# Twelve result stores begun by GpSimd in place of SyncE

## The chip, the cores and the metric

The kernel runs on one core of a Trainium2 chip. A core has five engines that each work through their own list of instructions in order: TensorE (PE in the profile), VectorE (DVE), ScalarE (ACT), GpSimd (POOL) and SyncE (SP). They meet at semaphores. The metric is device time in microseconds (us) of one execution.

## What is computed

Three stages follow one another. Attention through 32 memory slots for each of 4 batches and 8 heads gives `x`; a two-layer block with a sloped rectifier maps it; and a gated mixture of four experts, all of them evaluated, gives the result:

```
a    = softmax(phi);  k_m = a^T k;  v_m = a^T v            # per batch and head
attn = softmax(q k_m^T / 8) v_m                            # -> x, 2304 x 512
h    = x @ w_in;  g = max(h, 0) + alpha * min(h, 0);  x = g @ w_out
p    = domain_probs / sum(domain_probs)
for e in range(4):
    out += p[:, e] * (max(x @ w1[e], 0) @ w2[e])           # w1 512 x 1024, w2 1024 x 512
```

The result has 2304 rows (576 for each batch) and 512 columns, in float32.

## The kernel before

Products are done in three passes: each operand is split into a rounded high half and a low half (the rest), and high x high, high x low and low x high are summed. ScalarE makes the high half (a cast), VectorE or GpSimd the low half (a subtraction). So nearly every operand of TensorE passes two engines first. In a product of six matrix instructions the third and the sixth use the low half of the weights, the second and the fifth the low half of the other operand.

The expert stage cuts the four experts into eight groups `g` of 512 hidden columns, and takes batches in pairs: batches 0 and 1 for all eight groups, then batches 2 and 3. Both layers are done as 2 x 2 block products with seven multiplications in place of eight (Strassen's scheme). For the second layer (class `Seven`) a batch keeps seven sums P1 to P7 over all groups in SBUF, the tiles `acc`, and only at the end are these combined into the four blocks of the result: function `combine` (L1086 to L1097), seven additions of 128x576, of which four end in a block that is stored. Batches 0 to 2 store from `combine`, 288 KB a store, four for each batch; batch 3 ends in another form, and its eight stores of 144 KB come from `Down.flush` (L1018).

The order of all instructions is written out by hand in `ORDER` (L30), one name for a step; each engine gets its own steps in that order. `cb01` is the combination number 1 of batch 0; numbers 1, 4, 5 and 6 store. `ON_VECTOR` names the steps that VectorE does in place of GpSimd; of the combinations `cb03`, `cb11`, `cb14` and five of batch 3 are GpSimd's, the rest VectorE's. Batch 0 and batch 1 are combined between 727 and 773 us, interleaved with the first group of batches 2 and 3 and with the last group of batch 1; batch 2 at the end, between the last products of batch 3.

Names used below: `vl711` is the subtraction for the low half of the second-layer weight tile `w2711` of the last group; `D70_13` is a product of group 7, batch 0, that uses it (tile `c7013`). `x3l5` fills the low half of one of the seven first-layer operands of batch 3 (second half of tile `x36`), and `p4_030` uses it. `S02_4` is the difference for a second-layer operand of group 0, batch 2 (it is written to `h020`), `H02_4` and `H02_2` are casts (ScalarE), `L02_2` a subtraction, and `D02_4` the product behind them (tile `c024`). All subtractions of halves stand in one helper, so they carry its line, L324. The buffers of `acc` for batches 0 and 1 are used again for 2 and 3; the first write there waits until the stores have landed.

Of the kernel before, what the change touches and what calls it, by code (L numbers as in the profile page):

```python
# [288 lines left out]
def memory_attention_experts(ctx: ExitStack, tc: tile.TileContext, phi, q, kv, w_in, w_out, w1, w2, alpha, dp, out):  # L289


    nc = tc.nc
# [27 lines left out]
    def engine(name):  # L320
        return nc.vector if name in ON_VECTOR else nc.gpsimd
# [764 lines left out]
    def combine(b, n):  # L1086

        o, x, y, op = (
            (P6, P1, P6, ALU.add), (P2, P1, P2, ALU.add), (P7, P6, P7, ALU.add), (P6, P6, P5, ALU.add),
            (P3, P6, P3, ALU.add), (P4, P7, P4, ALU.subtract), (P5, P7, P5, ALU.add),  # L1090
        )[n]
        a = acc_t[b]
        engine(f"cb{b}{n}").tensor_tensor(out=a[o], in0=a[x], in1=a[y], op=op)
        if b < 3 and o in (P2, P3, P4, P5):
            i, j = divmod((P2, P3, P4, P5).index(o), 2)
            rows = out[i * 256:(i + 1) * 256, b * S + j * HB:b * S + (j + 1) * HB]
            nc.sync.dma_start(out=rows.rearrange("(m p) n -> p m n", p=128), in_=a[o])  # L1097

    def plan_experts():

# [76 lines left out]
        def do_combine(b, n):  # L1177
            do(f"cb{b}{n}", combine, b, n)
# [409 lines left out]
```

## Time and profile before

| | us |
|---|---|
| median of 3 runs | 1100.97 |
| lowest, highest | 1100.07, 1102.19 |
| the profiled execution | 1100.15 |
| its span, from first to last instruction | 1098.4 |

| engine | busy us | share |
|---|---|---|
| TensorE (PE) | 1089.1 | 99% |
| its weight loads (PEld) | 1055.4 | 96% |
| VectorE (DVE) | 804.6 | 73% |
| ScalarE (ACT) | 562.1 | 51% |
| GpSimd (POOL) | 548.3 | 50% |

The shares are means over the span. Transfers: 185.40 MB in 62584 packets, all issued by SyncE but for instruction fetches; the 16 DMA engines were busy for 47.9% with these. In the order of time a row is a run of like instructions on one engine: its start, the time from its first to its last, line, operation and tiles, their count, and in brackets how long the engine was idle before it and what ended that. SPq is SyncE's queue: only the issue is shown there, and the transfer goes on behind it.

### The profile page before, as it was taken

The page shows a single profiled execution, that of the slowest core. Times are in us where ns is not written, and L with a number is a line of the kernel's source. Part 1 is how long each engine was busy: PE and PEld are TensorE (multiplying, and loading weights), DVE is VectorE, ACT ScalarE, POOL GpSimd, SP SyncE. Part 2 cuts the span into 40 slices and gives each one's busy share as a digit, 9 for nine tenths or more (in the row PEclk, how much of TensorE's full clock was granted, in tenths as well). Part 3 has the DMA queues.
Part 4 walks back from the last instruction along what each step waited for, and adds up shares of the span by engine and source line. Part 5 has one row for each costly group of instructions (what it writes and reads, how often), then busy time and mean ns, then how long its engine had stood idle before and what let it go on. Part 6 is the DMA issues. An engine that isn't in the chain of part 4 may idle for free.

```text
span 1098.4 us, 22039 instructions
## 1 busy us (share of the span) xinstructions
PE 1089.1 (99%) x8550; PEld 1055.4 (96%) x8550; DVE 804.6 (73%) x1520; ACT 562.1 (51%) x1236; POOL 548.3 (50%) x443
## 2 busy tenths in 40 slices
PE   9999999999999999999999999999999999999998
PEld 8679999999999999999999999999999999999998
DVE  6987787767556778788788888888466666656556
ACT  5676654544444466665766666765523232333231
POOL 3656545533435466467665554544433333354572
PEclk9999999999999999999999999999999999999999
DMA  9930221201011438566646665778655564555542
GB/s 375 395 149 20 81 75 59 77 22 59 1 52 37 154 137 306 198 235 260 203 198 225 252 233 188 266 239 287 192 182 166 163 193 154 176 164 165 184 144 87
DMA packets 62584, 185.40 MB, mean 169 GB/s; under 512 B 6288, under 2 KB 24720, under 8 KB 58768
## 3 DMA queue, kind: packets, MB, share of 16 engines
q1 hardware_dynamic: 62480, 184.00, 47.9%
q8 instruction: 67, 1.10, 0.4%
q14 instruction: 37, 0.30, 0.1%
HBM read 117.62 MB, written 66.36 MB: 167 GB/s over the span
## 4 chain that ended last, share of the span: by engine, by line
PE 96%; DVE 2%; DMA 1%; issue 0%; SPq 0%; POOL 0%; ACT 0%; DVEq 0%; POOLq 0%
PE c L1064 30%; PE y L705 18%; PE uy L899 13%; PE uw L899 9%; PE ux L899 9%; PE h L671 9%; PE y L702 1%; PE pw L630 1%; PE warm L337 1%; PE o L1010 1%; PE pm L439 1%; PE h L668 1%; DMA w2c<-kS 1%; DMA w<-kw 1%; PE pc L471 0%; DVE h L1037 0%
## 5 line engine op out<-in xcount | busy, mean ns | idle before, releaser
L324 POOL TENSOR_TENSOR gc<-h,gc 128x576 fp32r<-128x576 f32 x102 | 149.5, 1473 | 204.7 <-ACT gc L1045 204.3
L705 PE MATMUL y<-g,wout 128*128 128x288 f32 x1440 | 205.5, 296 | 0.0
L705 PEld LDWEIGHTS y<-g,wout 128*128 128x128 f32 x1440 | 195.4, 188 | 7.3 <-ACT g L690 2.5
L1045 ACT CAST gc<-h 128x576 fp32r<-128x576 f32 x217 | 142.9, 674 | 115.0 <-DVE h L1037 69.8
L1064 PE MATMUL c<-gc,w2c 128*128 128x288 f32 x1260 | 192.3, 295 | 0.9 <-DMA w2c<-kS 0.9
L1084 DVE TENSOR_TENSOR acc<-c,acc 128x288 f32<-128x288 f32 x280 | 124.2, 453 | 83.5 <-PE c L1064 83.0
L899 PE MATMUL uy<-x,w 128*128 128x288 f32 x1152 | 183.1, 295 | 0.2 <-DMA w<-kw 0.2
L1064 PEld LDWEIGHTS c<-gc,w2c 128*128 128x128 f32 x1260 | 175.3, 188 | 1.3 <-ACT gc L1045 1.1
L899 PEld LDWEIGHTS uy<-x,w 128*128 128x128 f32 x1152 | 163.0, 188 | 0.4 <-ACT v L971 0.4
L324 POOL TENSOR_TENSOR g<-act,g 128x288 fp32r<-128x288 f32 x81 | 70.3, 875 | 123.6 <-ACT g L690 92.6
L899 PE MATMUL uw<-x,w 128*128 128x288 f32 x768 | 122.9, 296 | 0.2
L899 PE MATMUL ux<-x,w 128*128 128x288 f32 x768 | 121.7, 295 | 0.0
L1064 PE MATMUL c<-gc,sS 128*128 128x288 f32 x768 | 117.8, 295 | 1.1 <-DVE acc L1084 1.1
L671 PE MATMUL h<-a,wp 128*128 128x288 f32 x720 | 110.2, 296 | 0.0
L899 PEld LDWEIGHTS uw<-x,w 128*128 128x128 f32 x768 | 108.7, 188 | 0.9 <-DVE ux L936 0.6
L899 PEld LDWEIGHTS ux<-x,w 128*128 128x128 f32 x768 | 108.7, 188 | 0.0
L324 DVE TENSOR_TENSOR gc<-h,gc 128x576 fp32r<-128x576 f32 x115 | 100.5, 883 | 10.9 <-ACT gc L1045 10.7
L1064 PEld LDWEIGHTS c<-gc,sS 128*128 128x128 f32 x768 | 106.9, 188 | 1.4 <-DVE acc L1084 1.4
L686 DVE SCALAR_TENSOR_TENSOR act<-neg,bet,h 128x288 f32<-128x288 f32 x120 | 60.3, 510 | 63.9 <-ACT neg L677 57.4
L671 PEld LDWEIGHTS h<-a,wp 128*128 128x128 f32 x720 | 99.9, 188 | 5.7 <-issue 2.3
L677 ACT ACTIVATE neg<-h 128x288 f32<-128x288 f32 x128 | 52.1, 411 | 98.0 <-PE h L671 95.5
L1082 ACT COPY acc<-c 128x288 f32<-128x288 f32 x154 | 60.3, 401 | 75.1 <-PE c L1064 74.1
(160 smaller groups left out, 1618.3 us busy)
## 6 DMA issues: line engine op xcount, KB each, us to landing
kw<-w SPq DMA_DIRECT2D x16, 1792.0 KB, 8.2
raww<-in_w SPq DMA_DIRECT2D x32, 512.0 KB, 4.2
kS<-sS SPq DMA_DIRECT2D x32, 512.0 KB, 5.7
w<-kw SPq DMA_DIRECT2D x32, 512.0 KB, 4.8
w2c<-kS SPq DMA_DIRECT2D x32, 512.0 KB, 3.8
kw<-w SPq DMA_DIRECT2D x25, 512.0 KB, 5.9
w<-kw SPq DMA_DIRECT2D x48, 256.0 KB, 4.2
w2c<-kw SPq DMA_DIRECT2D x24, 512.0 KB, 3.7
```

What stands on the lines that cost most here:

```text
L324: eng.tensor_tensor(out=out, in0=in0, in1=in1.bitcast(F32), op=ALU.subtract)
L337: mm(p[:, 0:128], ident, ident, start=True, stop=True)
L439: mm(p[32 * h:32 * h + 32, 0:128], l, r, start=(c == 0), stop=(c == 4))
L671: mm(p, wp_t[b, c, g][:, x, fs], a_t[b][:, y, g, o:o + HB], start=(n == 0), stop=(n == 5))
L677: nc.scalar.activation(out=self.neg, in_=self.p, func=AF.Relu, scale=-1.0)
L686: nc.vector.scalar_tensor_tensor(out=self.g, in0=self.neg, scalar=bet[:, ft:ft + 1], in1=self.p, op0=ALU.mult, op1=ALU.add)
L705: mm(First.acc[d], w[:, x, d * 128:(d + 1) * 128], self.gt[:, y, 0:HB], start=(self.start and n == 0), stop=(self.stop and n == 2))
L899: mm(p, w[:, x, a, k], operand(self.b, i)[:, y, k], start=(start and n == 0), stop=(n == 5), skip_group_check=not start)
L1045: nc.scalar.copy(out=t[:, 0], in_=self.raw(q))
L1064: mm(p, w[:, x, i, m * 128:(m + 1) * 128], self.g_t[q][:, y, i], start=(fresh and k == 0), stop=(k == 5), skip_group_check=not fresh)
L1082: nc.scalar.copy(out=a, in_=self.ps[n])
L1084: nc.vector.tensor_tensor(out=a, in0=self.ps[n], in1=a, op=ALU.add)
```

## The change

One line of `combine`: the stores of the combined blocks are issued by GpSimd in place of SyncE. The steps, their order in `ORDER`, the additions and the bytes are the same.

```
@@ -1094,7 +1094,7 @@
         if b < 3 and o in (P2, P3, P4, P5):
             i, j = divmod((P2, P3, P4, P5).index(o), 2)
             rows = out[i * 256:(i + 1) * 256, b * S + j * HB:b * S + (j + 1) * HB]
-            nc.sync.dma_start(out=rows.rearrange("(m p) n -> p m n", p=128), in_=a[o])
+            nc.gpsimd.dma_start(out=rows.rearrange("(m p) n -> p m n", p=128), in_=a[o])
```

The order of instructions on GpSimd, first place: around the first store (`cb01`). `w2711` is the weight tile of `vl711`, `x30` an operand tile of batches 2 and 3, `acc0` the block that is stored.

```order
 L767 TENSOR_TENSOR xt23_9566<-yu211_9146,yu201_8524 128x576 [waits DVE_49,Pool_49]
 L1037 TENSOR_TENSOR h710_9369<-h711_9481,h710_9369 128x576 [waits DVE_49]
+L1097 DMA out_0<-acc0_5207 128x2x288 [waits DVE_49,Activation_49]
 L324 TENSOR_TENSOR w2711_9409<-raww215_9031,w2711_9409 128x512 [waits DMAHW1_49]
 L324 TENSOR_TENSOR x30_9604<-yu211_9146,x30_9604 128x576 [waits Activation_49]
```

The store, with its wait for VectorE's sum, now stands ahead of the subtraction for `w2711`.

GpSimd, second place: the other stores of batch 0 and the first of batch 1. `x36` is the tile of `x3l5`, the first `h020` row the difference `S02_4` or the one after it, `acc1` batch 1's block.

```order
 L1037 TENSOR_TENSOR h020_9674<-h020_9674 128x576 [waits DVE_49]
-L767 TENSOR_TENSOR xt32_9883<-yu310_9676,xt31_9798 128x576 [waits DMAHW4_49,DVE_49]
+L1097 DMA out_0<-acc0_5207 128x2x288 [waits DVE_49]
+L767 TENSOR_TENSOR xt32_9883<-yu310_9676,xt31_9798 128x576 [waits DMAHW3_49,Pool_49]
+L1097 DMA out_0<-acc0_5207 128x2x288 [waits DVE_49] x2
 L324 TENSOR_TENSOR x36_9863<-xt32_9883,x36_9863 128x576 [waits Activation_49]
+L1037 TENSOR_TENSOR h020_9674<-h021_9727,h020_9674 128x576
+L1093 TENSOR_TENSOR acc1_5524<-acc10_5525,acc1_5524 128x576
+L1097 DMA out_0<-acc1_5524 128x2x288 [waits Pool_49]
 L1037 TENSOR_TENSOR h020_9674<-h021_9727,h020_9674 128x576 [waits DVE_49]
```

Two stores in a row now stand ahead of `x36` and of the first of the two `h020` differences (`S02_4`).

SyncE, around the fourth and fifth stores: `w2c04` is the weight load with the row at 757.88 us.

```order
 L861 DMA w2c06_9936<-kw2011_5830 128x1024
-L1097 DMA out_0<-acc0_5207 128x2x288
 L827 DMA w170_8872<-kw110_5794 128x2x512
 L827 DMA w171_8992<-kw111_5895 128x2x512
 L827 DMA w170_8872<-kw110_5794 128x2x256
-L1097 DMA out_0<-acc1_5524 128x2x288
 L861 DMA w2c04_10018<-kS30_5751 128x1024
 L861 DMA w2c05_10086<-kS20_5159 128x1024
```

On SyncE the stores are gone, and the loads follow one another in the order that they had.

## Rows read from the trace of the kernel before

**Rows 1.** The page: busy us, share, instructions; the chain that ended last, by engine

```profile
PE 1089.1 (99%) x8550; PEld 1055.4 (96%) x8550; DVE 804.6 (73%) x1520; ACT 562.1 (51%) x1236; POOL 548.3 (50%) x443
...
PE 96%; DVE 2%; DMA 1%; issue 0%; SPq 0%; POOL 0%; ACT 0%; DVEq 0%; POOLq 0%
```

**Rows 2.** Waits of PE: who waited for whom, us in total, times, longest

```profile
PE warm L337 <- POOL ident masks.py:199: 1.4, 1, 1.4
...
PE c L1064 <- DVE acc L1084: 1.1, 1, 1.1
PE c L1064 <- DMA w2c<-kS: 0.9, 1, 0.9
```

**Rows 3.** Line L1097: ns least/median/most, first and last start us; landing

```profile
L1097 SPq EVENT_SEMAPHORE  x12: 17/17/7271, 721.4 to 1094.1; - x12
L1097 SPq DMA_DIRECT2D out<-acc x12: 378/388/541, 728.7 to 1094.4; - x12
...
DMA to landing us min/median/max: 2.3/2.7/7.0
```

**Rows 4.** Order of time, SyncE: start us, us, what

```profile
728.68 0.39 SPq L1097 DMA_DIRECT2D out<-acc  x1
...
757.88 1.05 SPq L861 DMA_DIRECT2D w2c<-kS  x2
...
1094.36 0.38 SPq L1097 DMA_DIRECT2D out<-acc  x1
1095.27 0.33 SPq L1018 DMA_DIRECT2D out<-acc  x1
```

**Rows 5.** Order of time, TensorE

```profile
727.01 1.75 PE L1064 MATMUL c<-gc,w 128*128 128x288 f32 x12
...
754.88 0.97 PE L899 MATMUL uy<-x,w 128*128 128x288 f32 x6
...
757.29 2.67 PE L1064 MATMUL c<-gc,w2c 128*128 128x288 f32 x18
...
765.63 1.03 PE L1064 MATMUL c<-gc,w2c 128*128 128x288 f32 x6 [0.92 <-DMA w2c<-kS]
...
776.03 1.75 PE L1064 MATMUL c<-gc,w2c 128*128 128x288 f32 x12
```

**Rows 6.** Order of time, GpSimd

```profile
721.85 1.81 POOL L324 TENSOR_TENSOR w<-raww,w 128x512 fp32r<-128x512 f32 x1
731.44 1.43 POOL L324 TENSOR_TENSOR x<-yu,x 128x576 fp32r<-128x576 f32 x1 [7.78 <-ACT x L775]
...
749.29 1.43 POOL L324 TENSOR_TENSOR x<-xt,x 128x576 fp32r<-128x576 f32 x1 [3.99 <-ACT x L775]
750.68 1.95 POOL L1037 TENSOR_TENSOR h<-h,h 128x576 f32<-128x576 f32 x1
...
769.56 2.01 POOL L1093 TENSOR_TENSOR acc<-acc,acc 128x576 f32<-128x576 f32 x1 [2.21 <-DVE acc L1093]
```

**Rows 7.** Order of time, VectorE

```profile
727.87 0.75 DVE L1093 TENSOR_TENSOR acc<-acc,acc 128x576 f32<-128x576 f32 x1
...
753.43 1.20 DVE L1093 TENSOR_TENSOR acc<-acc,acc 128x576 f32<-128x576 f32 x1
...
755.41 1.42 DVE L324 TENSOR_TENSOR gc<-h,gc 128x576 fp32r<-128x576 f32 x2
...
768.74 1.54 DVE L1093 TENSOR_TENSOR acc<-acc,acc 128x576 f32<-128x576 f32 x2
```

**Rows 8.** Order of time, ScalarE

```profile
753.78 1.25 ACT L1045 CAST gc<-h 128x576 fp32r<-128x576 f32 x2
...
775.64 0.41 ACT L1082 COPY acc<-c 128x288 f32<-128x288 f32 x1
```

**Rows 9.** DMA issues: count, KB each, median us to landing

```profile
out<-acc SPq DMA_DIRECT2D x8, 144.0 KB, 2.0
```

**Rows 10.** Cores: span, mean granted TensorE clock

```profile
core 0: 1098.4 us, clock 0.999
```

More of the change, by code (lines that the diff above doesn't have):

```diff
@@ L1096, in combine @@
             rows = out[i * 256:(i + 1) * 256, b * S + j * HB:b * S + (j + 1) * HB]
-            nc.sync.dma_start(out=rows.rearrange("(m p) n -> p m n", p=128), in_=a[o])
+            nc.gpsimd.dma_start(out=rows.rearrange("(m p) n -> p m n", p=128), in_=a[o])
     def plan_experts():
```

## The prediction

> **What bounds the kernel now.** I read the page's busy shares and chain of waits first, then TensorE's own waits, then the rows of the stores themselves, then the order of time on SyncE, GpSimd, TensorE, VectorE and ScalarE between 715 and 790 us and after 1090 us. TensorE (PE) is busy for 1089.1 of 1098.4 us and the chain that ends last is 96% PE [rows 1]. So hardly anything can be won: the one wait of PE near these stores is 0.92 us for a weight load, with 1.1 us for VectorE's accumulation before it [rows 2]. A microsecond that PE is made to wait is, on the other hand, nearly always a microsecond of the run, since no later stretch has slack to give it back. The reader should therefore ask what PE waits for, and nothing else.
>
> The twelve stores are cheap where they stand: SyncE (SP) needs 0.38 to 0.54 us to issue one, and they land after 2.3 to 7.0 us, median 2.7 [rows 3]. SP pays with waiting, up to 7.27 us for the first of them, because the block isn't summed yet [rows 3]; but SP only issues transfers and can afford it. In rows 4 the first store goes out at 728.68, right behind the VectorE sum that starts at 727.87 and takes 0.75 [rows 7]: 0.06 us from the end of the sum to the issue. That is my price for one hand-over from engine to engine.
>
> **What the move does.** GpSimd (POOL) works strictly in the order in which its instructions stand. A store put there waits for its sum, and all that stands behind it waits too. So for each of the twelve I asked which POOL instruction stands next and who needs it. Two figures are needed: the time of the sum, which the trace has, and the time for which POOL is held to begin a store, call it g, which it has not, since POOL issues no transfer before. The nearest rows are SP's 0.39 us for the same store [rows 3] and the 1.43 us of a POOL instruction over a block of this size [rows 6]; farther off lie 2.3 us, the shortest landing, if POOL were held till the data are out, and 0 if it only passed the order on. I take 1.0, near the middle of the two nearest, and keep 0.39 to 1.43 as the likely and 0 to 2.3 as the outer bounds. The Trainium skill, "DMA: Bandwidth & Descriptors", section "Specifications", gives about 1 us to the first byte by GpSimd's software path against about 0.6 us by SyncE's; no run here shows it, and by it the sum below would be the same.
>
> **Place 1, +3.5 us.** Behind the first store stands the subtraction that makes the low half of the second-layer weight tile w2711. Before, it ran at 721.85 for 1.81 us, and POOL then had nothing to do until 731.44 [rows 6]. Now it starts when the store has been issued: 728.68 + g, and ends at 730.49 + g. PE wants this tile in the second six of the twelve products at 727.01 [rows 5]; at 1.59/12 = 0.1325 us each (1.75 less the overlap of the last) the third of these six, the first to use the low half, was at 728.07. Wait: 728.68 + g + 1.81 + 0.06 - 728.07 = 2.48 + g = 3.48 us. VectorE's sum doesn't get earlier, since VectorE is busy ahead of it.
>
> **Place 2, +2.8 us.** The third and fourth stores stand directly before the subtraction for the last operand half of batch 3 (x36, before at 749.29) and the difference h020 (before at 750.68) [rows 6]. The fourth store's sum starts on VectorE only at 753.43 [rows 7]; without POOL beside it I give it 0.75 in place of 1.20, so it is done at 754.18, and POOL is through the store at 754.24 + g. Then x36 to 755.67 + g and h020 to 757.10 + g (1.43 each). PE wanted x36 in the third product from 754.88 on, at 755.14 [rows 5], so it waits 0.6 + g there. But the chain from h020 is longer: ScalarE's two casts (1.25 [rows 8]), of which the second doesn't need h020 but stands behind the one that does, VectorE's subtraction (0.71, half of a pair [rows 7]), three hand-overs: 759.24 + g. The products at 757.29 [rows 5] need it from their second on, at 757.42. Both waits together are 1.82 + g = 2.82 us. All this is in the times of before; sum and products shift alike by place 1, so it adds up.
>
> **Place 3, 0.** The stores of batch 1: VectorE's two sums end at 770.28 [rows 7], then store, POOL's own sum (2.01 before, at 769.56 [rows 6]; 1.43 without VectorE beside it) and its store. These land at 770.28 + 2g + 1.43 + (2.7 - 0.39) = 774.0 + 2g. ScalarE needs it at 775.64 [rows 8], as the buffer is written again there, and PE has 0.78 us to spare behind that (ScalarE's end at 776.05, second half of the products of 776.03 at 776.83 [rows 5]). Free up to g = 1.2; 0.5 us at g = 1.43.
>
> **What is saved, -0.9 us.** SP loses twelve issues and its waits. Of that only the 0.92 us at 765.63 [rows 5] reaches PE: the load for it is issued at 757.88 [rows 4], behind a store; now it has the 2.8 us of place 2 besides, so I count the wait as gone. What stands behind the first store in SP's queue (a weight copy, a gate row, weight loads) may go up to 7 us sooner, but PE waits for none of it now [rows 2], so that is worth nothing.
>
> **The end, +0.4 us.** Batch 2's stores find POOL idle. The last goes out at 1094.36 as before [rows 4], and lands at 1094.36 + 2.7 + (g - 0.39) = 1097.67, against 1095.27 + 2.0 = 1097.27 for the last of batch 3 [rows 3, 4, 9].
>
> **Sum**: 3.48 + 2.82 + 0 - 0.92 + 0.4 = 5.8 us on the profiled execution's 1100.15, so 1105.9. That run is 0.8 below the median of 1100.97; against that, 1106.8 us. With g = 0.39: 2.87 + 2.21 - 0.92 = 4.2, with 1.43: 3.91 + 3.25 + 0.5 - 0.92 + 0.8 = 7.5; that is 1105.1 to 1108.5 for the likeliest case.
>
> **A rule that would make g larger.** VectorE does only two-input sums and scaled products around both places, and these slow POOL somewhat: 1.81 to 2.01 us against 1.43 [rows 6]. The Trainium skill, "SBUF - State Buffer", section "Who interferes with whom", says that VectorE's copies, casts and one-input scalar operations can lock GpSimd out while it writes a transfer's descriptors, and that two-input sums don't. By the rule g stays short here. No run shows it yet.
>
> **Rivals.** (a) *Not slower*: the waiting store doesn't hold POOL's queue, or w2711 is somehow ready by 728.07; then nothing new waits, and SP's lighter queue takes away the 0.92: 1100.0. For it: POOL is idle half of the time [rows 1], and 7.8 us of it lie just there [rows 6]. Against: the idle time is behind w2711, and the store ahead of it. It decides at g + 1.81 + 728.68 < 728.07, which not even g = 0 meets. (b) *Held until landing*, g = 2.3: 4.78 + 4.12 + 2.2 - 0.92, and at the end four stores of 2.3 from 1090.2 on, landing near 1099.4 (+2.2): 12.4 us, 1113.4. For it speaks only that no row excludes it. (c) *The clock falls in the wait*. The granted clock is 0.999 in the mean [rows 10], and PE's waits are 1.4 us at most [rows 2]; 3.5 us in one piece don't occur. The missing 0.001 is 1.1 us over the run; one such loss at each place gives 5.8 + 2.2 = 8.0, 1109.0. The Trainium skill, "TensorE: Matmul & The Clock Gate", section "HAM oscillation", describes TensorE going back to 1.2 GHz when it has to wait for data; this trace shows no such case.
>
> **Chances.** Forecast (both waits, g up to 1.43) 0.72; (a) 0.10; (b) 0.08; (c) 0.10. The measurement tells about 0.2%, 2.2 us, from no change. Of the forecast hardly anything lies below that; of (a) most is "same". Faster 0.03, same 0.08, slower 0.89. The range takes in (c), part of (b), and below, g = 0 with a POOL subtraction of 1.43 in place 1 (2.1 + 1.8 - 0.9 = 3.0, 1104.0): 1103.5 to 1111.
>
> **What would show it.** In the changed profile PE waits for POOL's weight subtraction of w2711 (two to four us, nothing of it before), then near 755 + 3.5 us for POOL's x36 and for VectorE behind ScalarE; POOL's idle time before w2711 is put down to VectorE's sum; the wait for w2c at 765 is gone; the times after 790 are those of before plus a constant. It is wrong if w2711 still ends before its store, if a PE wait of this size shows at another place, or if POOL is held far off 1 us by a store.

## The result and the profile after

| | before | after |
|---|---|---|
| median us | 1100.52 (4 runs, 1099.91 to 1102.19) | 1110.09 (4 runs, 1109.28 to 1112.90) |
| the profiled execution | 1100.15 | 1109.79 |
| its span | 1098.4 | 1108.0 |

The ratio is 1.0094, interval 1.0081 to 1.0107. The kernel became slower by 9.6 us, where 5.8 were forecast.

First the page of the kernel after: busy us and share of each engine, and the chain that ended last (before: [rows 1]).

```profile
PE 1091.9 (99%) x8550; PEld 1057.2 (95%) x8550; DVE 808.9 (73%) x1520; ACT 562.4 (51%) x1236; POOL 556.2 (50%) x455
...
q0 software_dynamic: 960, 3.54, 0.9%
...
PE 93%; DVE 3%; issue 1%; DMA 1%; POOL 1%; ACT 0%; POOLq 0%; ACTq 0%; DVEq 0%
```

The twelve stores stand on POOL's list (455 in place of 443) and have a queue of their own (960 packets, 3.54 MB). The chain has given 3% of PE to DVE, POOL and DMA. PE's share says nothing, since a product at half clock counts as busy. PE's waits say more: five are new against [rows 2], of 3.58, 1.65, 0.39, 0.43 and 1.16 us, and the one for w2c of 0.92 us is gone. Where they stand is seen in the order of time on TensorE of the kernel after, with which [rows 5] are to be compared:

```profile
727.23 1.23 PE L1064 MATMUL c<-gc,w 128*128 128x288 f32 x8
732.04 1.20 PE L1064 MATMUL c<-gc,w 128*128 128x288 f32 x4 [3.58 <-POOL w L324]
...
737.38 0.96 PE L899 MATMUL uy<-x,w 128*128 128x288 f32 x6
...
762.43 0.94 PE L899 MATMUL uy<-x,w 128*128 128x288 f32 x5 [1.65 <-POOL x L324]
...
765.88 1.73 PE L1064 MATMUL c<-gc,w2c 128*128 128x288 f32 x11 [0.39 <-DVE gc L324]
768.03 1.07 PE L1064 MATMUL c<-gc,w2c 128*128 128x288 f32 x6 [0.43 <-ACT acc L1082]
768.93 0.96 PE L899 MATMUL uy<-x,w 128*128 128x288 f32 x6
...
784.02 0.96 PE L1064 MATMUL c<-gc,w2c 128*128 128x288 f32 x6
786.14 1.06 PE L1064 MATMUL c<-gc,w2c 128*128 128x288 f32 x6 [1.16 <-ACT acc L1082]
787.04 0.96 PE L899 MATMUL uy<-x,w 128*128 128x288 f32 x6
```

The same three products behind the places on TensorE of the kernel before:

```profile
731.78 0.96 PE L899 MATMUL uy<-x,w 128*128 128x288 f32 x6
...
759.79 0.95 PE L899 MATMUL uy<-x,w 128*128 128x288 f32 x6
...
777.62 0.96 PE L899 MATMUL uy<-x,w 128*128 128x288 f32 x6
```

The sum of the difference is read from such rows: the start of the same product in both traces, at each place. The profiled run of after was 0.22 us late already at 727.23. After that it lost 5.38 us by 737.38 (before 731.78), 3.54 more by 768.93 (before 759.79), gave back 1.15 by 784.02 (before 776.03), where the wait for w2c was, and lost 1.43 by 787.04 (before 777.62). It won 0.37 where PE of the kernel before waits 0.15 us for a weight load, at 1044.14. The end is 0.55 longer: the last issue at 1104.32 is followed by 3.68 us, before by 3.13. Together 0.22 + 5.38 + 3.54 - 1.15 + 1.43 - 0.37 + 0.55 = 9.6.

The windows of the kernel after around place 1 (the stretch, its length, busy us of PE, PEld, DVE, ACT and POOL with their counts, PE's granted clock, DMA share, GB/s) show what the rows of PE alone don't tell:

```profile
730.00:732.00 2.00, 0.00 (x0) 0.00 (x0) 1.22 (x3) 0.00 (x0) 1.97 (x2) 1.00 0.57 147
732.00:734.00 2.00, 1.96 (x8) 1.96 (x9) 0.00 (x0) 0.69 (x2) 0.00 (x0) 0.55 0.98 373
734.00:736.00 2.00, 2.00 (x11) 2.00 (x11) 0.00 (x0) 0.45 (x3) 0.00 (x0) 0.59 0.09 37
736.00:738.00 2.00, 2.00 (x17) 2.00 (x16) 0.42 (x1) 2.00 (x4) 0.95 (x1) 1.00 0.03 8
```

After the wait PE runs for some 3.7 us mostly at the lower of its two levels, 1.2 GHz: 8 and 11 products in 2 us where 17 are usual. Of the 5.38 us of place 1, 3.75 are the wait (the ninth product was due at 727.23 + 8 x 0.1325 = 728.29 and began at 732.04) and 1.63 the clock.

GpSimd in the kernel after, around the first store, the fourth, and the last two of batch 1 (before: [rows 6]):

```profile
729.53 0.87 POOL L1097 DMA_DIRECT2D out<-acc  x1 [7.42 <-DVE h L1037]
730.42 1.57 POOL L324 TENSOR_TENSOR w<-raww,w 128x512 fp32r<-128x512 f32 x1
...
760.21 0.73 POOL L1097 DMA_DIRECT2D out<-acc  x1 [3.62 <-DVE ux L936]
760.97 1.41 POOL L324 TENSOR_TENSOR x<-xt,x 128x576 fp32r<-128x576 f32 x1
762.32 1.43 POOL L1037 TENSOR_TENSOR h<-h,h 128x576 f32<-128x576 f32 x1
...
779.46 0.72 POOL L1097 DMA_DIRECT2D out<-acc  x1 [1.82 <-DVE acc L1093]
780.21 1.45 POOL L1093 TENSOR_TENSOR acc<-acc,acc 128x576 f32<-128x576 f32 x1
782.06 0.73 POOL L1097 DMA_DIRECT2D out<-acc  x1 [0.41 <-POOL acc L1093]
```

w2711 is subtracted behind the store, and the operand of `x3l5` behind the fourth. The line of the stores in the kernel after (before: [rows 3]) gives what GpSimd needs for one, and how long they took to land:

```profile
L1097 POOL DMA_DIRECT2D out<-acc x12: 725/725/872, 729.5 to 1103.8; - x12
...
DMA to landing us min/median/max: 2.6/3.0/7.3
```

ScalarE waited for two of them, in the order of time of the kernel after (before: [rows 8]):

```profile
767.58 0.40 ACT L1082 COPY acc<-c 128x288 f32<-128x288 f32 x1 [2.55 <-DMA out<-acc]
...
785.69 0.40 ACT L1082 COPY acc<-c 128x288 f32<-128x288 f32 x1 [0.73 <-DMA out<-acc]
```

At these two rows the block buffer of batch 0 (of batch 1) is written for the first time by batch 2 (batch 3). Three of the four stored blocks, those of the numbers 1, 4 and 5, lie in one tile (`Seven.flush`, L1076 to L1079), so this write waits until all three stores have landed. The fourth store of batch 0, begun at 760.21, landed 7.27 us later; the last of batch 1 (`cb14`), begun at 782.06, 3.53 us later. Both stand in the chain of waits:

```profile
760.21 7.27 DMA out<-acc
...
782.06 3.53 DMA out<-acc
```

### The profile page after: what moved, and what is told of

It is laid out like the page before. It is cut to its first block, busy times and chain, and to the rows that moved or that the text cites. A ratio compares the mean times of both kernels' runs of the same rounds, so it can differ in the third digit from the quotient of the medians.

```text
span 1108.0 us, 22038 instructions
## 1 busy us (share of the span) xinstructions
PE 1091.9 (99%) x8550; PEld 1057.2 (95%) x8550; DVE 808.9 (73%) x1520; ACT 562.4 (51%) x1236; POOL 556.2 (50%) x455
## 3 DMA queue, kind: packets, MB, share of 16 engines
q0 software_dynamic: 960, 3.54, 0.9%
## 4 chain that ended last, share of the span: by engine, by line
PE 93%; DVE 3%; issue 1%; DMA 1%; POOL 1%; ACT 0%; POOLq 0%; ACTq 0%; DVEq 0%
PE c L1064 29%; PE y L705 17%; PE uy L899 13%; PE uw L899 9%; PE ux L899 9%; PE h L671 9%; PE y L702 1%; PE pw L630 1%; PE warm L337 1%; PE pm L439 1%; DMA out<-acc 1%; PE h L668 1%; DVE gc L324 1%; PE pc L471 0%; DVE acc L1093 0%
## 5 line engine op out<-in xcount | busy, mean ns | idle before, releaser
L324 DVE TENSOR_TENSOR gc<-h,gc 128x576 fp32r<-128x576 f32 x115 | 103.4, 908 | 13.7 <-ACT gc L1045 13.3
```

Of the source, the lines that this page charges most:

```text
L324: eng.tensor_tensor(out=out, in0=in0, in1=in1.bitcast(F32), op=ALU.subtract)
```

## Experiments

Theory A says that a store costs by its place: by what stands behind it on GpSimd while it waits, by the clock after a long wait, and by its landing. Rival B says that a store that GpSimd begins costs about 0.8 us wherever it stands (9.6 / 12). Shifts are read as above, from the same product in two traces; ratios are against the kernel before. Executions start the stretch at 727 us up to 1.0 us apart, so spans alone tell less than shifts.

**The first store back on SyncE.**

```
-            nc.gpsimd.dma_start(out=rows...., in_=a[o])
+            eng = nc.sync if (b, n) == (0, 1) else nc.gpsimd
+            eng.dma_start(out=rows...., in_=a[o])
```

> Only the first store (cb01 of batch 0) goes back to SyncE, the other eleven stay on GpSimd. Theory A (position): a store costs what stands behind it in GpSimd's queue while it waits for its sum; the first one costs 5.4 us of the 9.6 in the profiled runs (3.6 of wait for w2711, the rest at a lower granted clock). So about +4.2 us against before, ratio near 1.0038, no wait of PE for w2711, and granted clock 1.00 in 730 to 740. Rival B (each store has a price of its own, 0.8 us, wherever it stands): +8.8 us, ratio 1.0080.

Measured: ratio 1.0033 (1.0021 to 1.0045), span 1102.4. The shift at place 1 is 0 (731.70 against 731.78), the clock 1.00 throughout. This is as A says.

**The first store alone on GpSimd** (the condition above with `!=`).

> Only the first store is begun by GpSimd, the other eleven by SyncE. A: the whole of place 1, about +5.4 us, ratio near 1.0049, with the wait for w2711 of 3.6 us and the lower clock behind it, nothing at places 2 and 3, and the 0.9 us wait for w2c at 765 still there or hidden by the shift. B: +0.8 us, ratio 1.0007.

Measured: ratio 1.0042 (1.0029 to 1.0055), span 1102.9. One store of twelve costs nearly half of the loss, and B is out. TensorE of this run, and its windows behind the wait:

```profile
731.92 1.06 PE L1064 MATMUL c<-gc,w 128*128 128x288 f32 x4 [3.58 <-POOL w L324]
...
737.26 0.96 PE L899 MATMUL uy<-x,w 128*128 128x288 f32 x6
```

```profile
732.00:734.00 2.00, 2.00 (x10) 2.00 (x11) 0.00 (x0) 0.95 (x3) 0.00 (x0) 0.57 1.05 400
734.00:736.00 2.00, 2.00 (x11) 2.00 (x11) 0.00 (x0) 0.30 (x2) 0.00 (x0) 0.58 0.02 8
```

The stretch began at 727.11, 0.10 late, so the shift by 737.26 is 5.38, as in the kernel after. Of the w2c wait 0.4 us is left.

**The subtraction ahead of the store**, all twelve on GpSimd; in `ORDER`:

```
- ... p6_020 cb01 sk7S3 x3h0 p1_021 S71_6 E70_13 D71_1 F71_1 E71_5 vl711 pg03 D70_13 ...
+ ... p6_020 vl711 cb01 sk7S3 x3h0 p1_021 S71_6 E70_13 D71_1 F71_1 E71_5 pg03 D70_13 ...
```

> All twelve stores are on GpSimd; in the list of steps only the subtraction vl711 is moved ahead of cb01, so that w2711 is made before the store waits. A: place 1 disappears as in the run with the first store on SyncE, about +4.2 us against before (ratio 1.0038), though GpSimd still begins the store. B (or the time of beginning a store is what counts): no change from the changed kernel, +9 us or more.

Measured: ratio 1.0038 (1.0025 to 1.0050), no wait for w2711, clock 1.00. GpSimd still begins the store, and place 1 is free: its price was the order alone.

**Work for TensorE during the wait.** `p5_021` ahead of `D70_13`, and five times over:

```
-            self.product(self.w, V1, T1, True)
+            for _ in range(5 if self.name == "021" else 1):
+                self.product(self.w, V1, T1, True)
```

> All stores on GpSimd as in the changed kernel; the product p5_021 is moved ahead of D70_13 and done five times over (24 more matrix instructions, about 3.2 us, the last pass gives the result), so that PE has work while GpSimd is held by the first store. If the lower clock behind place 1 comes from PE's idle time: the granted clock stays at 1.00 from 730 to 740, the shift against before at 738 to 760 is 3.4 to 4.0 us in place of 5.6, and the run about 8 us over before (1.0073). If the clock falls for another reason (GpSimd's or VectorE's work, the transfer): the low stretch stays, and the run is at least as slow as the changed kernel, 9.6 us or more.

Measured: ratio 1.0076 (1.0062 to 1.0090), span 1106.2, 1.8 us under the kernel after although 24 products more are done; the intervals of the two ratios overlap, so the trace decides. The windows of this run:

```profile
730.00:732.00 2.00, 2.00 (x17) 2.00 (x17) 0.89 (x2) 0.00 (x0) 1.66 (x2) 1.00 0.66 174
732.00:734.00 2.00, 1.86 (x14) 1.63 (x13) 0.00 (x0) 1.31 (x4) 0.00 (x0) 1.00 0.97 375
734.00:736.00 2.00, 2.00 (x17) 2.00 (x16) 0.56 (x2) 2.00 (x5) 1.22 (x1) 1.00 0.05 14
```

GpSimd's store and subtraction are done as in the kernel after (1.66 us of GpSimd in 730 to 732, DMA share 0.66 and 0.97 there and behind); only PE isn't idle, and the clock stays at 1.00. The stretch began at 726.90, 0.11 early, so the shift is 3.57 us, of which 24 x 0.1325 = 3.18 are the added products; the other 0.39 us I can't put down to anything. So the 1.63 us of clock come from PE's idle time.

**Batch 2's four stores alone on GpSimd** (condition `b < 2` for SyncE).

> Only batch 2's four stores, at the end, are begun by GpSimd; the eight of batches 0 and 1 stay on SyncE. A (position): nothing stands behind them that PE waits for, so only the later landing of the last one counts: +0.2 to +0.6 us, ratio 1.0000 to 1.0006, and all times up to 1090 us as before. B (a price for each store, 0.8 us): +3.2 us, ratio 1.0029.

Measured: ratio 1.0006 (0.9997 to 1.0015), no new wait of PE. This is as A says; B's 1.0029 is outside.

**The third and fourth stores back on SyncE** (`cb04`, `cb05` of batch 0).

> The third and fourth stores (cb04 and cb05 of batch 0) go back to SyncE, ten stay on GpSimd. A: place 2 goes, with PE's waits for x36 (1.65 us), for VectorE's gc (0.39) and for ScalarE's acc (0.43): 3.5 us less than the changed kernel, of which up to 1.1 us may come back as the wait for w2c that the changed kernel has lost; +6 to +7.2 us against before (1.0055 to 1.0065). B (0.8 us a store): +8 us (1.0073). If the wait for ScalarE's acc stays, the fourth store lands late because of the traffic and not because GpSimd began it.

Measured: ratio 1.0065 (1.0052 to 1.0078), the upper end of A. B's 1.0073 lies in the interval too, so here the trace decides. PE's waits for x36, gc and ScalarE's acc at 762 to 768 are gone; 0.18 us of the w2c wait came back, and a new wait of 0.60 stands at 758.54, which hangs on VectorE (its two subtractions at 751.41 took 3.19 us; see the run with five stores). The fourth store, on SyncE ahead of the weight loads again, landed after 2.4 us.

**The last two stores of batch 1 back on SyncE** (`cb16`, `cb14`).

> The last two stores of batch 1 (cb16 and cb14) go back to SyncE, ten stay on GpSimd. A: place 3 is paid because GpSimd begins both stores in turn with its own sum between them, so that the last one lands too late for ScalarE's next write of that block; without it PE's wait of 1.16 us near 786 goes, and the run is 1.0 to 1.4 us shorter than the changed kernel's, about +8.3 us against before (1.0075), places 1 and 2 unchanged. Rival: the landing is late because the transfers are crowded by then, whoever begins them: the wait stays, +9 to +9.6 us.

Measured: ratio 1.0073 (1.0060 to 1.0087). PE's wait near 786 is gone, places 1 and 2 stand (3.57 and 1.65 us). That is what A says; the times alone don't exclude the rival, whose 9 us are 1.0082. VectorE's two sums ran as late in this run as in the kernel after (778.09 against 777.49, in a run that was 0.60 later at the product of 768.03), so their lateness alone doesn't make the wait: GpSimd's holding of the two stores is needed for it. Why they are late is seen on VectorE of the kernel before and of the kernel after, just ahead of them:

```profile
764.64 1.42 DVE L324 TENSOR_TENSOR gc<-h,gc 128x576 fp32r<-128x576 f32 x2
...
773.79 2.55 DVE L324 TENSOR_TENSOR gc<-h,gc 128x576 fp32r<-128x576 f32 x2
```

In each run in which GpSimd begins the store of `cb15` in its place, a subtraction of GpSimd stands right behind it (773.60 in the kernel after), and these two of VectorE take 2.44 to 2.56 us; in each run in which SyncE begins it they take 1.42.

**All stores behind the work that PE waits for**, as steps of their own on GpSimd: in `ORDER` `st01` behind `vl711`, `st06` behind `x3t2`, `st04 st05 st11` behind `cb11`, `st15` behind `L02_6`, `st16 st14` behind `cb14`.

```
+    def store(b, n):
+        ...
+        nc.gpsimd.dma_start(out=rows...., in_=acc_t[b][o])
```

> All twelve stores on GpSimd, but as steps of their own, each behind the GpSimd work that PE waits for: the first behind vl711, the third and fourth behind x3l5, S02_4 and cb11, those of batch 1 behind the next operand work. A: GpSimd may begin the stores if nothing waits behind them: the waits of places 1 and 2 go, with at most 1.5 us left where a store that goes out later also lands later before ScalarE's next write of its block: 0 to +1.5 us against before (1.0000 to 1.0014). B (the beginning of a store costs as such): +5 us or more.

Measured: ratio 1.0055 (1.0043 to 1.0068), and this I had wrong. The waits of places 1 and 2 did go, but later stores landed later, and at 780.70 PE waited another 0.74 us for VectorE's gc. ScalarE and TensorE of this run:

```profile
763.27 0.40 ACT L1082 COPY acc<-c 128x288 f32<-128x288 f32 x1 [7.41 <-DMA out<-acc]
...
763.72 1.06 PE L1064 MATMUL c<-gc,w2c 128*128 128x288 f32 x6 [3.86 <-ACT acc L1082]
```

The fourth store stands in the chain of waits of this run:

```profile
755.90 7.27 DMA out<-acc
```

Why it took so long is told by SyncE of the kernel before, in the order of time, where the fourth store and the fifth stand on either side of three weight loads:

```profile
754.65 0.39 SPq L1097 DMA_DIRECT2D out<-acc  x1
755.15 2.04 SPq L827 DMA_DIRECT2D w<-kw  x3
757.29 0.54 SPq L1097 DMA_DIRECT2D out<-acc  x1
```

The store ahead of the loads landed after 3.6 us, at 758.25, just before ScalarE's write at 758.43; the one behind them after 7.0, and the sixth, behind three more loads, after 6.4. In the kernel after, and in this run, SyncE doesn't wait for the sum any more and sends the loads first (from 758.75 in after, the store at 760.21; from 753.97 here, the store at 755.90).

**The loads ahead of the store, all on SyncE** (kernel before; `wr100 wr113 wr105` ahead of `cb05`).

> The kernel before, all stores on SyncE; in the list of steps only the three weight loads wr100, wr113, wr105 (line L827, 2.04 us of issue) are moved ahead of the store of cb05. Theory T (traffic): in the changed kernel the store of cb05 took 7.3 us to land, and 3.6 before, because SyncE no longer waits for its sum and lets these loads go first. Then here too, with the store on SyncE, it lands after about 7 us, ScalarE's first write to the block buffer waits for it (before it started at 758.43) and PE loses 3 to 4.5 us: ratio 1.0027 to 1.004. Rival Q: the landing is slow because GpSimd's queue is slow beside SyncE's transfers; then a store on SyncE still lands after 3.6 to 4.5 us, and the run is +0 to +0.9 us (1.0000 to 1.0008).

The move was too coarse: the loads also went past `p6_031` and `p2_031`, which should still read the columns before, so this kernel doesn't compute the result. PE waited 8.13 us for the loads, and the ratio of 1.0071 says nothing of the question. The landing can be read: stores on SyncE, begun at 756.13 behind the three loads, landed after 7.5 and 7.8 us, as T said. And stores that GpSimd began with no loads right ahead landed fast: after 2.7 and 2.6 us the second and third of the kernel after. So the long landing belongs to the traffic ahead, not to GpSimd's queue; what it alone costs in time this run doesn't show.

**Five stores on GpSimd, in the places that looked free** (`cb01` with `vl711` ahead, `cb06`, `cb04`, `cb11`, `cb15`).

> Five stores on GpSimd (cb01 with vl711 moved ahead of it, cb06 and cb04 of batch 0, cb11 and cb15 of batch 1), seven on SyncE: cb05, cb16, cb14 and the four of batch 2. If the prices found so far are those of places (first store ahead of w2711, fifth block's store ahead of x36 and h020, last two of batch 1, the end), none is left: -0.9 to +0.6 us against before, ratio 0.9992 to 1.0005, with PE's waits after 727 us at most 0.9 us. If beginning a store on GpSimd has a price of its own (0.8 us): +4 us, ratio 1.0036.

Measured: ratio 1.0029 (1.0019 to 1.0038); a miss again. A price of 0.8 us for each store, 1.0036, would fit this time, so it is the trace and the next run that tell. This run, in the order of time, on GpSimd, VectorE and TensorE:

```profile
746.76 0.73 POOL L1098 DMA_DIRECT2D out<-acc  x1 [3.10 <-DMA w2c<-kS]
747.51 1.44 POOL L767 TENSOR_TENSOR xt<-yu,xt 128x576 f32<-128x576 f32 x1
...
751.29 1.44 POOL L324 TENSOR_TENSOR x<-xt,x 128x576 fp32r<-128x576 f32 x1
752.67 1.41 POOL L1037 TENSOR_TENSOR h<-h,h 128x576 f32<-128x576 f32 x1
754.03 1.39 POOL L1093 TENSOR_TENSOR acc<-acc,acc 128x576 f32<-128x576 f32 x1
...
746.38 3.20 DVE L324 TENSOR_TENSOR x<-yu,x 128x576 fp32r<-128x576 f32 x2
...
751.70 4.35 DVE L324 TENSOR_TENSOR x<-xt,x 128x576 fp32r<-128x576 f32 x1
...
756.11 2.57 PE L899 MATMUL uy<-x,w 128*128 128x288 f32 x11 [3.04 <-DVE x L324]
```

VectorE of the kernel before at the same two places:

```profile
746.10 1.43 DVE L324 TENSOR_TENSOR x<-yu,x 128x576 fp32r<-128x576 f32 x2
...
749.82 1.52 DVE L324 TENSOR_TENSOR x<-xt,x 128x576 fp32r<-128x576 f32 x1
```

The stores of `cb06` and `cb04` push GpSimd's instructions behind them onto VectorE's subtractions. These took 1.43 (two of them) and 1.52 us; now 3.20 and 4.35, the latter through three GpSimd instructions in a row. The Trainium skill, "SBUF - State Buffer", section "Who interferes with whom", says that a VectorE instruction with two inputs in SBUF and a GpSimd instruction that reads SBUF block each other, the second waiting for the first. The rows agree with the blocking. That the one begun at 751.70 also stood through two GpSimd instructions that started after it, at 752.67 and 754.03, the page doesn't say. In the kernel before it came in behind the first of the same three, and the second took 1.95 us [rows 6] in place of 1.41; what decides between the two is not shown.

**Three stores on GpSimd** (the same without `cb06` and `cb04`).

> Only three stores on GpSimd: cb01 with vl711 moved ahead of it, cb11 and cb15 of batch 1; the other nine on SyncE, cb06 and cb04 among them. In the run with five, PE lost 3.0 us at 756 to a subtraction of VectorE (line L324, 4.35 us in place of 1.52) that ran beside three GpSimd instructions in a row, which the stores of cb06 and cb04 had pushed later. If these two stores are the cause, GpSimd's instructions stand at 743 to 754 where they stood before, the subtraction takes about 1.5 us again, the wait of 3.0 us goes, and the run is -0.9 to +0.4 us against before (0.9992 to 1.0004). Rival: it is the store of cb11, or GpSimd's beginning of stores as such, that holds VectorE up: the wait stays, +2.5 to +3.5 us (1.0023 to 1.0032).

Measured: ratio 1.0000 (0.9991 to 1.0009), span 1098.4. Both instructions of VectorE are back to 1.43 and 1.52 us, PE's wait of 3.0 us is gone, and two small ones of 0.6 and 0.3 stand in place of the 0.9 for w2c.

**The load earlier, without the change** (kernel before; `cl04` right behind `cb05`).

> The kernel before, all stores on SyncE; in the list of steps only the weight load cl04 (w2c04) is moved from behind the first store of batch 1 to right behind the store of cb05. It is what the change gives back at 765 us, without the change: the wait of 0.92 us for w2c goes, -0.9 us, ratio 0.9992 (less than the times can tell; the wait in the trace tells it). If the three loads that now go out 0.55 us later are wanted then, or another load becomes the last, 0 or slower by up to 0.5 us.

Measured: ratio 0.9993 (0.9984 to 1.0002), span 1097.3. The wait for w2c is gone and PE has no new one. The times can't tell this from no change; by the trace it is what the changed kernel gives back, with no new wait for it. Its ratio is the lowest of the versions tried, but the times don't tell it from that with three stores.

## Why the prediction came out as it did

The direction, places 1 and 2 and their order were right: PE's waits for w2711, then for x36 and behind VectorE's gc. The prices of all three places were too small. Of the 3.8 us between forecast and result 1.6 are the clock at place 1, 1.4 are place 3 and 0.7 the landing of the fourth store, all three left out of the sum; the rest is small and of both signs. That 1110.09 still lies within 1103.5 to 1111 is in part luck: the likeliest case ended at 1108.5, and the range was made wider for rivals (b) and (c), of which only the clock of (c) came true, at one place.

- **Place 1, +3.5; measured 5.38.** The wait itself was nearly right: 3.75 against 3.48. GpSimd held the store 0.87 us, not 1.0, but began it only 0.6 us after its release (728.9 by its semaphore row, 729.53), and the subtraction took 1.57, not 1.81. What failed is that I counted the wait alone as the price and left the clock to rival (c). The rival was right here: 1.63 us (1.1 in my text). That PE had run no such wait in the kernel before was in the text, and it should have raised the chance, not lowered it. The Trainium skill, "TensorE: Matmul & The Clock Gate", section "HAM oscillation", describes the return to 1.2 GHz when PE waits for data; the granted clock of 0.55 and 0.59 behind the wait agrees. At place 2, with 1.65 us in one piece, the clock stayed at 1.00.
- **Place 2, +2.8; measured 3.54.** PE waited 1.81 us for x36 against 1.6 (762.43, due at 760.62); it wanted it in the second of the six products, not in the third as I counted. The chain from h020 came as worked out: the product behind it began at 765.88 and was due at 763.02 (757.42 and the 5.60 of shift by then), 2.86 us against 2.82. What failed is the landing of the fourth store, which I put at nothing: behind VectorE's gc PE met ScalarE's acc (0.43 us idle), held by that landing, and lost the other 0.68 us. I had looked at the reuse of the buffer for batch 1 only, while batch 0 had 0.2 us to spare in the kernel before.
- **Place 3, 0; measured 1.43.** Three things were mis-sized. The median landing of 2.7 stood for this store's 3.53. A store holds GpSimd for more than the 0.73 us of its row: from the end of a sum to the next instruction 760.97 - 759.79 = 1.18 at `cb05` (VectorE's sum is done at 759.79), 782.82 - 781.66 = 1.16 at `cb14`. And VectorE's two sums ran 8.75 us late there (777.49 against 768.74) while PE, which had its 1.15 us back, ran 7.99 late, 0.75 less; the store of `cb15` had pushed GpSimd's work onto VectorE's just ahead of them. With these my own sum is 770.28 + 0.75 + 1.17 + 1.43 + 0.41 + 3.53 = 777.57, against 775.64 when ScalarE wants it and 0.78 to spare: 1.15 us, and PE's wait is 1.16.
- **Saved, -0.9; measured -1.15**, as said. But "worth nothing" for what stands behind the stores on SyncE was wrong: there was a cost, since the loads that SyncE now sends sooner stand ahead of the fourth store, which landed after 7.27 us in place of 3.6.
- **The end, +0.4; measured 0.55.** Right.
- Rival (a) is out: what stands behind a waiting store did wait. Rival (b) is out: g is far from 2.3.

The price of places 1 and 2 together with the end is shown by single runs (first store alone 1.0042; third and fourth back, 1.0094 to 1.0065). That place 3 needs the last two stores of batch 1 on GpSimd is shown too (with both back the wait is gone); how its 1.43 us split between the holding, the landing and the late sums is worked out, not tried singly. How much of place 2 the traffic alone would cost is not shown.

## What to carry to other kernels

Ask of a transfer that is moved to a computing engine what stands behind it there, how late its data are, and who waits for that; the issue itself (0.73 us here) is the small part. Ask next what the relieved queue will do sooner: here its waiting had kept weight loads behind a store that was wanted early. And where TensorE is the bound, a wait of several microseconds in one piece is to be priced with the slow stretch behind it, here 1.6 us on 3.75.

## What the runs showed of the hardware

The granted clock fell to the lower of its two levels with four waits of PE: 0.55 and 0.59 in the two slices of 2 us behind 3.58 us, 0.69 and 0.50 behind 3.86 (stores as steps of their own), 0.66 and 0.50 behind 3.04 (five stores), and 0.50 during and behind 8.13 (loads ahead); behind 1.65 us it stayed at 1.00. A store of 288 KB occupied GpSimd for 0.73 us (0.87 the first), and 1.2 with its hand-overs, against 0.39 on SyncE. It landed after a median of 3.0 us against 2.7. The stores begun right behind three weight loads between 754 and 766 us landed after 6.4 to 8.1 us from either engine (kernels before and after, stores as steps of their own, loads ahead); the other stores of the kernel before took 2.3 to 4.3 us. VectorE's subtraction of 128x576 took up to 4.35 us in place of 0.75 undisturbed, beside three GpSimd instructions that followed each other without a gap.
